# Two-scale attention with a top-1 expert layer: attention issued as a software pipeline over head pairs

## The chip, the cores and the metric

The kernel runs on one core of a Trainium2 chip. The metric is the device time of one execution in microseconds (us). The core has five engines with queues of their own: PE (matmuls; the loads of its stationary operand are listed as PEld), DVE and ACT (elementwise work, both reach PSUM), POOL (elementwise work on SBUF and indirect DMA) and SP (here only DMA issue). Each engine executes its own instructions in order and waits for others through semaphores.

## The reference

Inputs: q, k, v of shape 8 batches x 8 heads x 576 positions x 64, and the weights of 8 experts. Per head there are two attentions: one over sequences pooled by 4 (144 positions, full softmax), repeated by 4, and one local, in which a position sees the 7 positions around it. Their sum, as 4608 tokens of 512 channels, goes through a top-1 expert layer.

```python
q_d = q.reshape(B, H, Sd, 4, D).mean(axis=3)            # k_d, v_d likewise, Sd = 144
out_up = np.repeat(sm_attn(q_d, k_d, v_d), 4, axis=2)
mask = np.abs(pos[:, None] - pos[None, :]) < 4
scores = np.where(mask, scale * np.matmul(q, k.transpose(0, 1, 3, 2)), -1e9)
x = out_up + np.matmul(softmax(scores), v)              # then (B*S, H*D) = (4608, 512)
e_idx = np.argmax(x @ w_gate, axis=1)
h = np.maximum(x[mask] @ w1[e], 0.0); ye = h @ w2[e]
out[mask] = gate_w[mask, None] * sigmoid(x @ w_output_gate)[mask, e, None] * ye
```

## The kernel before

**Two stages.** The attention stage takes batches one after the other and, in a batch, 4 head pairs; after its last pair a batch is gated: its tokens are given an expert and a rank there and are scattered by indirect DMA to a buffer in HBM, `hx_xs`, with one region per expert. The expert stage then reads each region back (`xg`), transposes it, and runs two matmuls per expert. `hx_xs` is filled beforehand with zero rows from the tile `zt`, since the expert stage always reads 640 rows.

**A pair (attn_pair).** q and k of two heads are loaded (`f`), cast to fp16 on POOL (`s16`, line 177), and transposed on PE into PSUM (`tp`, L180); the same operand times a small pooling matrix `pb` gives the pooled q and k (`pool_ps`, L182). Copies bring both to SBUF (`sT` on DVE, L185; `qkd` on ACT, L188). Scores are computed transposed, keys on partitions. A matmul with the identity first writes the additive mask (`mk`) into PSUM (L195 with 456 columns in `pa`, L209 with 408 columns in `pbt`), then the q.k matmuls add to it (L199; L211, L213, L215). These have 64 contraction rows, since head 0 lies on partitions 0 to 63 and head 1 on 64 to 127. So a head has 864 score columns: 576 local and 2 x 144 pooled.

**Exp in two halves.** To keep near-fp32 precision with fp16 matmuls, exp is taken twice on ACT, once to fp32 (`E`, L217 and L219) and once to fp16 (`eh`, L218 and L220), and `el`, the difference of the two, is formed on POOL for head 0 (L222) and on DVE for head 1 (L224). v is split likewise into `vh` (POOL, L345) and `vl` (DVE, L346), for a whole batch ahead of its pairs. The pooled v (`pd`, L353) is the product of `pv` and these: 12 matmuls of 512 columns per batch.

**Values.** Per head, 27 matmuls of 64 or 65 columns accumulate into `po`: 5 local blocks (L231) times (eh.vh, eh.vl, el.vh), and two pooled blocks (L238), each over two key chunks, of 128 and of 16 contraction rows, times the same three products. The 65th column carries the row sum of the softmax; DVE takes its reciprocal (L243) and scales into `xo` (L244).

**Gate (once per batch).** Pooled rows are repeated by 6 DMAs from `xo` to `up` (L253, L256); DVE adds them (L258), ACT casts to `t_xh` (L259), POOL forms the low half `t_xl` (L260). PE transposes both for each of 5 token blocks (L265, L267), DVE copies (`xT`, L269), PE forms the logits `lg` (L271, L274); a chain of small operations on DVE and ACT gives positions (L278 to L328), and POOL issues 5 scatters (L330).

**What sets the order.** The program is written straight down, loop by loop; a list scheduler then orders the instructions of each engine from the program's order, its own estimates and the free buffers of the pools, and puts in the waits. [...]

## Time and profile before

| what | value |
|---|---|
| runs shown | 784.08, 785.86, 788.26 us; median 785.86 |
| the profiled execution's own time | 780.59 us |
| its span, first to last instruction | 778.8 us |
| busy: PE, DVE, ACT, POOL | 514.8, 289.9, 216.4, 334.8 us |
| mean granted clock of PE | 0.657 of full speed |
| first addition of `up` (L258) for batch 0, for batch 7 | 98.9 and 570.6 us |
| first transposes of the expert stage (L390) | 604.32 us |

The span is cut at the three last times: a beginning with the first batch, seven batches of equal build, the end of the last gate, and the expert stage. Engine times in the table are sums of instruction times; instructions of one engine can overlap on PE, where matmuls are pipelined, so there the distance from one start to the next is what counts. Where an engine is idle, the views say what it waited for.

### The profile page before, as it was taken

The page shows a single profiled execution, that of the slowest core. Times are in us where ns is not written, and L with a number is a line of the kernel's source. Part 1 is how long each engine was busy: PE and PEld are TensorE (multiplying, and loading weights), DVE is VectorE, ACT ScalarE, POOL GpSimd, SP SyncE. Part 2 cuts the span into 40 slices and gives each one's busy share as a digit, 9 for nine tenths or more (in the row PEclk, how much of TensorE's full clock was granted, in tenths as well). Part 3 has the DMA queues.
Part 4 walks back from the last instruction along what each step waited for, and adds up shares of the span by engine and source line. Part 5 has one row for each costly group of instructions (what it writes and reads, how often), then busy time and mean ns, then how long its engine had stood idle before and what let it go on. Part 6 is the DMA issues. An engine that isn't in the chain of part 4 may idle for free. (4 is left out here: it accounts for less than half of the span.)

```text
span 778.8 us, 12008 instructions
## 1 busy us (share of the span) xinstructions
PE 514.8 (66%) x4849; PEld 326.8 (42%) x4849; DVE 289.9 (37%) x577; ACT 216.4 (28%) x441; POOL 334.8 (43%) x269
## 2 busy tenths in 40 slices
PE   1339636946772793777379378547711999799994
PEld 1116324615542461453345156335411655455552
DVE  4015434444443544454354345242322222222220
ACT  0124114413321441332144133223310233233331
POOL 9235466714924662491476346026122133233222
PEclk9855555555565655555555555655555899899997
DMA  9999664471424235143332414201022289889411
GB/s 204 244 228 203 129 125 107 81 153 26 110 63 88 75 72 122 46 110 71 76 80 67 88 34 90 64 1 31 21 45 75 55 184 194 196 168 199 138 61 69
DMA packets 152562, 81.66 MB, mean 105 GB/s; under 512 B 121709, under 2 KB 140141, under 8 KB 152496
## 3 DMA queue, kind: packets, MB, share of 16 engines
q1 hardware_dynamic: 129584, 44.52, 27.5%
q0 software_dynamic: 17664, 30.98, 18.8%
q10 hardware_dynamic: 5248, 5.28, 2.3%
q8 instruction: 40, 0.66, 0.3%
q14 instruction: 26, 0.21, 0.1%
HBM read 68.23 MB, written 20.72 MB: 114 GB/s over the span
## 5 line engine op out<-in xcount | busy, mean ns | idle before, releaser
L345 POOL TENSOR_SCALAR t_vh<-vf 128x640 f16<-128x640 f32 x32 | 68.5, 2142 | 98.1 <-DMA f<-in_k_dram 64.3
L177 POOL CAST s<-f 96x768 f16<-96x768 f32 x64 | 66.1, 1045 | 98.7 <-PE pool_ps L182 59.2
L265 PE MATMUL tp<-id,t_xh 128*128 128x128 f16 x160 | 22.2, 303 | 100.1 <-ACT t_xh L259 100.1
L231 PE MATMUL po<-t_vh,el 128*128 128x65 f16 x320 | 57.5, 243 | 34.9 <-POOL el L222 34.2
L399 PE MATMUL pu<-xgT,w1sb 128*128 128x320 f16 x512 | 73.7, 306 | 1.8 <-DVE xgT L391 1.5
L260 POOL TENSOR_TENSOR t_xl<-xo,t_xh 120x2560 f16<-120x2560 f32 x8 | 40.2, 5028 | 71.4 <-ACT t_xh L259 60.1
L409 PE MATMUL py<-w2sb,hs 128*128 128x512 f16 x320 | 70.4, 379 | 0.0
L222 POOL TENSOR_TENSOR el<-E,eh 128x864 f16<-128x864 f32 x32 | 58.4, 1826 | 20.1 <-ACT eh L220 19.4
L412 POOL DMA_INDIRECT out_dram<-y,xg x40 | 39.2, 980 | 63.5 <-ACT y L411 61.7
L231 PE MATMUL po<-t_vh,eh 128*128 128x65 f16 x320 | 61.0, 244 | 7.6 <-ACT eh L218 6.7
L231 PEld LDWEIGHTS <-eh 128*128 128x128 f16 x640 | 54.6, 130 | 19.7 <-ACT eh L218 8.7
L238 PE MATMUL po<-vd1h,el 128*128 128x65 f16 (+1 forms) x256 | 62.0, 242 | 0.0
L238 PE MATMUL po<-vdl,eh 128*128 128x64 f16 (+1 forms) x256 | 61.5, 240 | 0.0
L180 PE MATMUL tp<-id,s 96*128 96x96 f16 x384 | 39.2, 255 | 33.6 <-POOL s L177 33.6
L399 PEld LDWEIGHTS <-w1sb 128*128 128x128 f16 x512 | 51.3, 100 | 23.4 <-issue 2.8
L231 PE MATMUL po<-vl,eh 128*128 128x64 f16 x320 | 60.7, 242 | 0.0
L238 PE MATMUL po<-vd1h,eh 128*128 128x65 f16 (+1 forms) x256 | 60.1, 235 | 0.0
L231 PEld LDWEIGHTS <-el 128*128 128x128 f16 x320 | 41.5, 130 | 40.9 <-POOL el L222 38.6
L217 ACT ACTIVATE E<-pa 128x456 f32<-128x456 f32 x64 | 35.8, 559 | 80.4 <-PE pa L199 50.1
L265 PEld LDWEIGHTS <-t_xh 128*128 128x128 f16 x160 | 14.3, 132 | 103.8 <-ACT t_xh L259 103.8
L185 DVE COPY sT<-tp 128x576 f16<-128x576 f16 x64 | 29.0, 454 | 64.4 <-PE tp L180 49.3
L330 POOL DMA_INDIRECT hx_xs<-t_xh,pos x40 | 43.2, 1080 | 20.5 <-issue 10.4
(117 smaller groups left out, 1035.1 us busy)
## 6 DMA issues: line engine op xcount, KB each, us to landing
vf<-in_v_dram SPq DMA_DIRECT2D x64, 160.0 KB, 3.4
f<-in_q_dram SPq DMA_DIRECT2D x64, 144.0 KB, 3.3
f<-in_k_dram SPq DMA_DIRECT2D x64, 144.0 KB, 3.4
w1sb<-in_moe_w_dram POOLq DMA_DIRECT2D x8, 1024.0 KB, 10.6
w2sb<-in_moe_w_dram POOLq DMA_DIRECT2D x8, 1024.0 KB, 11.0
up<-xo SPq DMA_DIRECT2D x32, 240.0 KB, 4.4
hx_xs<-zt ACTq DMA_DIRECT2D x8, 645.0 KB, 16.0
xg<-hx_xs SPq DMA_DIRECT2D x8, 645.0 KB, 4.9
```

Of the source, the lines that this page charges most:

```text
L177: nc.gpsimd.tensor_copy(s16, f.rearrange("p m h d -> p m (h d)"))
L180: nc.tensor.transpose(tp[:, 96 * m:96 * m + 96], s16[:, m, :], id16[0:96, 0:96])
L222: nc.gpsimd.tensor_tensor(el, E32, eh, op=ALU.subtract)
L231: mm = nc.tensor.matmul(po[:, t, 0:n], lhsT=a[:, c], rhs=bm[:, hh, t, 0:n], start=(a is eh and bm is vh), stop=(a is el), skip_group_check ...
L238: mm = nc.tensor.matmul(po[:, g, 0:n], lhsT=a[0:kn, c], rhs=bm[0:kn, kc, hh, 0:n], start=(kc == 0 and a is eh and bm is vdh), stop=(kc == ...
L260: nc.gpsimd.tensor_tensor(xl[0:BR], x, xh[0:BR, :, 0:Dm], op=ALU.subtract)
L265: nc.tensor.transpose(tp[:, c, :], xh[:, t, 128 * c:128 * c + 128], id16)
L330: ins = nc.gpsimd.indirect_dma_start(out=xs_dram.ap(), out_offset=bass.IndirectOffsetOnAxis(ap=pos[:, t:t + 1], axis=0), in_=xh[0:P, t, :] ...
L345: nc.gpsimd.tensor_scalar(vh[:, hs, :, 0:D], vf, scalar1=VS, scalar2=None, op0=ALU.mult)
L399: nc.tensor.matmul(pu[:, 0:c1 - c0], lhsT=w1sb[:, c, 128 * f:128 * f + 128], rhs=xgT[:, c, c0:c1], start=(c == 0), stop=(c == 3))
L409: nc.tensor.matmul(py, lhsT=hs[:, f, 128 * j:128 * j + 128], rhs=w2sb[:, f, :], start=(f == 0), stop=(f == NG - 1))
L412: ins = nc.gpsimd.indirect_dma_start(out=out_rows, out_offset=bass.IndirectOffsetOnAxis(ap=xgi[:, j, Dm // 2 + 1:Dm // 2 + 2], axis=0), in ...
```

## The change

The attention stage is rewritten over 32 units, a unit being a pair of heads. `load(u)` issues the loads and the casts, `prep(u)` splits v, transposes and pools q and k and pools v, `scores_a` and `scores_b` compute the 456 and the 408 score columns of both heads together, with the head in the inner loop, into a double bank each (tags SA and SB, one buffer), and `soft` follows them. The main loop issues, for unit u, the loads of u+3, the scores of u+1, the values of u and the preparation of u+2; the gate is cut into `gate1`, `gate2` and `gate3`, issued after the first, second and third unit of the next batch.

- In `soft`, exp to fp16 goes to `eh`, then exp to fp32 is written back in place into PSUM, and DVE subtracts `eh` from it. One instruction covers both heads (912 and 816 columns). The tile `E` and POOL's subtraction are gone.
- `vh` is formed on ACT. v is pooled per unit: 12 matmuls of 128 columns, and the second one's output has 128 rows in place of 16.
- In `values`, all products with `eh` come first, then those with `el`, so both key chunks of the pooled blocks are gone through twice per head.
- In the gate the addition of `up` goes from DVE to POOL, and two of five copies `xT` go to ACT. In the last batch it is done block by block.
- `tp`, `lg`, `rk`, the pooled v and both outputs of the transposes share the two banks of tag T.
- The fill of `hx_xs` goes from ACT's queue to SP's, behind the loads of the fourth unit. The weights of experts 0 to 2 are requested after units 10, 16 and 22, with a copy of one element that makes the request wait for that unit.

The expert stage is the same.

```diff
-    pv = cst.tile([128, NB, SD], F16)
+    pv = cst.tile([128, NB, 256], F16)
...
-    for r in range(E):
-        nc.scalar.dma_start(
...
+    def prefill():
+        for r in range(E):
+            nc.sync.dma_start(
+                xs_dram.ap()[r * REG:r * REG + 128 * CAPJ, :].rearrange("(j p) d -> p j d", p=128),
+                _ap(zt, [zt.ap[0], [0, CAPJ], [1, XW // 2]]))
...
+    def load_weights(e, after=None):
         w1sb = wpool.tile([128, 4, F], F16, tag="w1")
+        w2sb = wpool.tile([128, NG, Dm], F16, tag="w2")
+        if after is not None:
+            nc.gpsimd.tensor_copy(w1sb[0:1, 0, 0:1], after)
+            nc.gpsimd.tensor_copy(w2sb[0:1, 0, 0:1], after)
...
-    def attn_pair(b, hp, vh, vdh, vdl, xo, vl):
...
+    def load(u):
+        b, hp = u // NP, u % NP
+        s16 = []
         for i, src in enumerate((q, k)):
             f = sbA.tile([96, 6, 2, D], F32, tag=f"qk{i}", bufs=3)
             for h in range(2):
+                nc.sync.dma_start(f[:, :, h, :], src[b, 2 * hp + h].rearrange("(m p) d -> p m d", p=96))
+            t16 = sbA.tile([96, 6, 2 * D], F16, tag=f"qk16{i}")
+            nc.gpsimd.tensor_copy(t16, f.rearrange("p m h d -> p m (h d)"))
+            s16.append(t16)
+        vf = sbA.tile([128, 2, NB, D], F32, tag="vf", bufs=3)
+        for h in range(2):
+            s = v[b, 2 * hp + h]
+            nc.sync.dma_start(vf[:, h, :, :], _ap(s, [[D, 128], [W * D, NB], [1, D]]))
+        st[u] = {"s16": s16, "vf": vf}
+
+    def prep(u):
+        d = st[u]
+        s16, vf = d.pop("s16"), d.pop("vf")
+        vh = vh_s[u % 3]
+        vl = sbA.tile([128, 2, NB, D], F16, tag="vl", bufs=3)
+        nc.scalar.activation(vh[:, :, :, 0:D], vf, AF.Copy, scale=VS)
+        nc.vector.scalar_tensor_tensor(vl, in0=vf, scalar=VS, in1=vh[:, :, :, 0:D],
+                                       op0=ALU.mult, op1=ALU.subtract)
+        qkT = sbA.tile([128, 2 * S], F16, tag="qkT", bufs=3)
+        t1 = psA.tile([128, 1024], F16, tag="T", bufs=2)
+        t2f = psA.tile([128, 512], F32, tag="T", bufs=2)
+        t2 = t2f.bitcast(F16)
+        n1 = 960
+        for i in range(2):
             for m in range(6):
+                c = S * i + 96 * m
+                o = t1[:, c:c + 96] if c < n1 else t2[:, c - n1:c - n1 + 96]
+                nc.tensor.transpose(o, s16[i][:, m, :], id16[0:96, 0:96])
+        for i in range(2):
             for m in range(6):
+                c = 96 + SD * i + 24 * m
+                nc.tensor.matmul(t2f[:, c:c + 24], lhsT=s16[i][:, m, :], rhs=pb[0:96, 0:24],
+                                 start=True, stop=True)
+        nc.vector.tensor_copy(qkT[:, 0:n1], t1[:, 0:n1])
+        nc.vector.tensor_copy(qkT[:, n1:2 * S], t2[:, 0:2 * S - n1])
+        qkd = sbA.tile([128, 2 * SD], F16, tag="qkd", bufs=3)
+        nc.scalar.copy(qkd, t2f[:, 96:96 + 2 * SD])
+        vdh = vdh_s[u % 3]
+        vdl = sbA.tile([128, 2, 2, D], F16, tag="vdl", bufs=3)
+        pd = psA.tile([128, 2, 2, D], F32, tag="T", bufs=2)
+        mms = [(t, m) for t in range(NB) for m in (vh, vl)]
+        for i, (t, m) in enumerate(mms):
+            nc.tensor.matmul(pd[:, 0], lhsT=pv[:, t, 0:128], rhs=m[:, :, t, 0:D],
+                             start=(i == 0), stop=(i == len(mms) - 1), skip_group_check=True)
+        for i, m in enumerate((vh, vl)):
+            nc.tensor.matmul(pd[:, 1], lhsT=pv[:, NB - 1, 128:256], rhs=m[:, :, NB - 1, 0:D],
+                             start=(i == 0), stop=(i == 1), skip_group_check=True)
+        nc.scalar.copy(vdh[:, :, :, 0:D], pd)
+        nc.vector.tensor_tensor(vdl, pd, vdh[:, :, :, 0:D], op=ALU.subtract)
+        d.update(qT=qkT[:, 0:S], kT=qkT[:, S:2 * S], qd=qkd[:, 0:SD], kd=qkd[:, SD:2 * SD],
+                 vh=vh, vl=vl, vdh=vdh, vdl=vdl)
+        d["eh"] = sbA.tile([128, 2, ND], F16, tag="eh", name="eh", bufs=2)
+        d["el"] = sbA.tile([128, 2, ND], F16, tag="el", name="el", bufs=2)
+
+    def soft(d, ps, c0, c1):
+        n = c1 - c0
+        nc.scalar.activation(d["eh"][:, :, c0:c1], ps[:, :, 0:n], AF.Exp, scale=scale)
+        nc.scalar.activation(ps[:, :, 0:n], ps[:, :, 0:n], AF.Exp, scale=scale)
+        nc.vector.tensor_tensor(d["el"][:, :, c0:c1], ps[:, :, 0:n], d["eh"][:, :, c0:c1], op=ALU.subtract)
+    def scores_a(u):
+        d = st[u]
+        ps = psA.tile([128, 2, 512], F32, tag="SA")
         for h in range(2):
+            nc.tensor.matmul(ps[:, h, 0:NA], lhsT=id16, rhs=mk[:, 0:NA], start=True, stop=False,
                              skip_group_check=True)
+        for t in range(4):
+            for h in range(2):
+                r = slice(64 * h, 64 * h + 64)
+                nc.tensor.matmul(ps[:, h, Q0[t]:Q0[t] + QN[t]], lhsT=d["kT"][r, W * t:W * t + 128],
+                                 rhs=d["qT"][r, Q0[t]:Q0[t] + QN[t]], start=False, stop=True,
                                  skip_group_check=True)
+        soft(d, ps, 0, NA)
+    def scores_b(u):
+        d = st[u]
+        ps = psA.tile([128, 2, 512], F32, tag="SB")
         for h in range(2):
+            nc.tensor.matmul(ps[:, h, 0:NBt], lhsT=id16, rhs=mk[:, NA:ND], start=True, stop=False,
+                             skip_group_check=True)
+        for c0, c1, kk, k0, k1, qq in ((0, 120, "kT", W * 4, W * 4 + 128, d["qT"][:, NA:S]),
+                                       (120, 120 + SD, "kd", 0, 128, d["qd"]),
+                                       (120 + SD, NBt, "kd", 128, SD, d["qd"])):
+            for h in range(2):
+                r = slice(64 * h, 64 * h + 64)
+                nc.tensor.matmul(ps[0:k1 - k0, h, c0:c1], lhsT=d[kk][r, k0:k1], rhs=qq[r],
+                                 start=False, stop=True, skip_group_check=True)
+        soft(d, ps, NA, ND)
+
+    def values(u, h, xo):
+        d = st[u]
+        eh, el = d["eh"][:, h], d["el"][:, h]
+        hh = 2 * (u % NP) + h
+        po = psA.tile([128, NB + 2, 65], F32, tag="O", bufs=2)
+        mms = []
+        for e_, hi in ((eh, True), (el, False)):
             for t in range(NB):
                 c = slice(Q0[t], Q0[t] + 128)
+                mms.append((po[:, t, 0:65], e_[:, c], d["vh"][:, h, t, 0:65]))
+                if hi:
+                    mms.append((po[:, t, 0:D], e_[:, c], d["vl"][:, h, t, :]))
             for g, q0 in ((NB, 0), (NB + 1, 16)):
                 for kc, kn in ((0, 128), (1, 16)):
                     c = slice(S + SD * kc + q0, S + SD * kc + q0 + 128)
+                    mms.append((po[:, g, 0:65], e_[0:kn, c], d["vdh"][0:kn, kc, h, 0:65]))
+                    if hi:
+                        mms.append((po[:, g, 0:D], e_[0:kn, c], d["vdl"][0:kn, kc, h, :]))
+        for i, (o, a, m) in enumerate(mms):
+            nc.tensor.matmul(o, lhsT=a, rhs=m, start=(i == 0), stop=(i == len(mms) - 1),
+                             skip_group_check=True)
...
-    def gate(b, xo):
+    def gate1(b, parts):
...
-        nc.vector.tensor_tensor(x, x, up, op=ALU.add)
+        for t0, t1 in parts:
+            x = xo[0:BR, t0:t1, :]
+            nc.gpsimd.tensor_tensor(x, x, up[:, t0:t1], op=ALU.add)
+            nc.scalar.copy(xh[0:BR, t0:t1, 0:Dm], x)
+            nc.gpsimd.tensor_tensor(xl[0:BR, t0:t1], x, xh[0:BR, t0:t1, 0:Dm], op=ALU.subtract)
+    def gate2(b, ts):
+        xh, xl = xh_s[b % 2], t_xl
+        if ts[0] == 0:
+            lg_s[b] = psA.tile([128, NB, 4 * E], F32, tag="T", name="lg", bufs=2)
+        lg = lg_s[b]
+        for t in ts:
             tp = psA.tile([128, 8, 128], F16, tag="T", bufs=2)
             for c in range(4):
                 nc.tensor.transpose(tp[:, c, :], xh[:, t, 128 * c:128 * c + 128], id16)
             for c in range(4):
                 nc.tensor.transpose(tp[:, 4 + c, :], xl[:, t, 128 * c:128 * c + 128], id16)
             xT = sbA.tile([128, 8, 128], F16, tag="xT")
+            if t % 2:
+                nc.scalar.copy(xT, tp)
+            else:
+                nc.vector.tensor_copy(xT, tp)
...
+    def gate3(b):
...
-        rk = psA.tile([128, NB, E], F32, tag="M")
+        rk = psA.tile([128, NB, E], F32, tag="T", bufs=2)
...
+    xo_s, lg_s = {}, {}
+    NU = B * NP
+    late = {10: 0, 16: 1, 22: 2}
+    def late_weights(u):
+        if u in late:
+            load_weights(late[u], st[u]["vh"][0:1, 0, 0, 0:1])
+    for u in range(3):
+        load(u)
+    for u in range(2):
+        prep(u)
+    scores_a(0)
+    scores_b(0)
+    for u in range(NU + 5):
+        b, hp = u // NP, u % NP
+        if u == 1:
+            prefill()
+        if u + 3 < NU:
+            load(u + 3)
+        if u + 1 < NU:
+            scores_a(u + 1)
+        if u < NU:
+            if hp == 0:
+                xo_s[b] = sbA.tile([128, NB + 2, Dm], F32, tag="xo", name="xo")
+            values(u, 0, xo_s[b])
+        if u + 1 < NU:
+            scores_b(u + 1)
+        if u + 2 < NU:
+            prep(u + 2)
+        if u < NU:
+            values(u, 1, xo_s[b])
+            late_weights(u)
+        gb = b - 1
+        last = gb == B - 1
+        if gb >= 0:
+            if hp == 0:
+                gate1(gb, [(t, t + 1) for t in range(NB)] if last else [(0, NB)])
+            if (hp == 1 and not last) or (hp == 0 and last):
+                gate2(gb, [0, 1, 2, 3, 4])
+            if (hp == 2 and not last) or (hp == 0 and last):
+                gate3(gb)
+            if last:
+                break
```

The scheduler makes of this, at three places, the following. First PE, at the end of a batch. Before, behind the last values (`po`) come the pooled v of the next batch (`pd`) and then the gate's transposes (`tp`):

```order
L353 MATMUL pd_2545<-vl_2523,pv_102 128x512
L353 LDWEIGHTS pv_102
L353 MATMUL pd_2558<-t_vh_142,pv_102 16x512
L353 LDWEIGHTS pv_102
L353 MATMUL pd_2558<-vl_2523,pv_102 16x512
L265 LDWEIGHTS t_xh_135
L265 MATMUL tp_2364<-id16_61,t_xh_135 128x128
```

Now the first transposes of the gate of batch 3 stand between the values of units 18 and 19, four units after their batch, and values follow them at once:

```order
L298 MATMUL po_3846<-t_vd_135,el_3427 128x65
L331 LDWEIGHTS t_xh_152
L331 MATMUL tp_3629<-id16_61,t_xh_152 128x128
L331 LDWEIGHTS t_xh_152
L331 MATMUL tp_3629<-id16_61,t_xh_152 128x128
L331 LDWEIGHTS t_xh_152
L331 MATMUL tp_3629<-id16_61,t_xh_152 128x128
L331 LDWEIGHTS t_xh_152
L331 MATMUL tp_3629<-id16_61,t_xh_152 128x128
L298 LDWEIGHTS eh_3595
L298 MATMUL po_3964<-t_vh_137,eh_3595 128x65
```

So what PE waited for at a batch's end is asked for a batch later. Second, POOL around a gate. Before, the low half (L260), the scatters (L330) and the subtractions for exp (L222) stand between the casts:

```order
L222 TENSOR_TENSOR el_2267<-E32_2265,eh_2266 128x864
L345 TENSOR_SCALAR t_vh_133<-vf_3318 128x10x64
L260 TENSOR_TENSOR t_xl_151<-xo_1780,t_xh_135 120x2560
L177 CAST s16_2854<-f_2851 96x768
L330 DMA hx_xs<-t_xh_135,pos_2502 36864x258 x5
L222 TENSOR_TENSOR el_2621<-E32_2619,eh_2620 128x864
```

Now the subtractions are gone, the addition (L319) has come, and between the gate of one batch and the scatters of it lie five casts:

```order
L319 TENSOR_TENSOR xo_3332<-xo_3332,up_4244 120x2560
L187 CAST t16_4257<-f_4254 96x768
L321 TENSOR_TENSOR t_xl_159<-xo_3332,t_xh_145 120x2560
L187 CAST t16_4262<-f_4259 96x768
L187 CAST t16_4506<-f_4503 96x768
L187 CAST t16_4511<-f_4508 96x768
L187 CAST t16_4725<-f_4722 96x768
L187 CAST t16_4730<-f_4727 96x768
L402 DMA hx_xs<-t_xh_145,pos_4705 36864x258 x5
```

A cast that stands behind an addition or a scatter waits for it. Third, the beginning. Before, ACT's queue opens with the fill, ahead of everything that ACT computes:

```order
L145 DMA hx_xs<-zt 128x5x258 x8
L355 ACT_TABLE_LOAD
L355 CAST vd1h<-pd 128x8x64
L355 CAST vd1h<-pd 16x8x64
L188 CAST qkd<-pool_ps 128x288
L217 ACTIVATE E_270<-pa 128x456
```

Now it stands in SP's queue, behind the loads of the fourth unit and ahead of those of the fifth:

```order
L192 DMA vf<-in_v_dram 128x5x64 x2
L149 DMA hx_xs<-zt 128x5x258 x8
L185 DMA f<-in_q_dram 96x6x64 x2
L185 DMA f<-in_k_dram 96x6x64 x2
L192 DMA vf<-in_v_dram 128x5x64 x2
```

ACT's queue begins with its own work, and the loads from the fifth unit on are issued after the fill.

125 lines of the change are left out of this document (18 added, 107 removed).

## The prediction

> **What bounds the kernel now.** I first cut the span into stages. The columns are the stretch in us, its length, the busy time of PE, PEld, DVE, ACT and POOL (instructions in brackets), the granted clock of PE, the DMA share and GB/s.
>
> ```profile
> 98.90:570.60 471.70, 304.94 (x3359) 200.70 (x3359) 204.34 (x407) 138.35 (x292) 229.08 (x146) 0.56 0.35 75
> 570.60:604.30 33.70, 6.57 (x87) 5.68 (x88) 9.21 (x28) 3.06 (x4) 10.05 (x6) 0.50 0.18 52
> 604.30:778.80 174.50, 155.25 (x992) 93.83 (x992) 44.61 (x88) 55.49 (x104) 47.98 (x50) 0.94 0.63 140
> ```
>
> The cuts are the first and the last addition of the gate and the first transposes of the experts. Seven batches take 471.7 us, 67.4 each. In these PE is busy for 304.9 / 7 = 43.6, POOL 32.7, DVE 29.2, ACT 19.8. So no engine is full: PE idles 24 us per batch. The view of waits says for what:
>
> ```profile
> PE tp L265 <- ACT t_xh L259: 100.1, 8, 15.7
> ...
> PE tp L180 <- POOL s L177: 33.6, 6, 10.8
> ```
>
> These are 134 us, the beginning and the last batch included: the gate, 100.1 / 8 = 12.5 per batch, and the preparation behind it. PE stands at the gate's transposes, and nothing of the next batch is put ahead of them. The experts (174.5 us) are PE at nearly full clock and stay.
>
> **The clock decides what PE's work costs.** Inside a batch there are long stretches without idle time, and they run at half clock:
>
> ```profile
> 535.50:556.00 20.50, 20.43 (x232) 13.86 (x233) 8.46 (x17) 8.98 (x20) 8.59 (x7) 0.50 0.01 2
> ```
>
> It rises only where one dense piece fills some 3 us, such as the gate's transposes and logits, and goes again:
>
> ```profile
> 248.60:252.00 3.40, 3.04 (x48) 2.78 (x46) 2.01 (x4) 0.00 (x0) 0.00 (x0) 0.50 0.00 0
> 252.00:255.40 3.40, 2.79 (x63) 2.23 (x59) 3.05 (x9) 0.47 (x2) 0.00 (x0) 1.00 0.00 0
> ```
>
> [...] After the change the two dense pieces get thinner: the pooled v shrinks from 12 matmuls of 512 columns to 12 of 128, and the gate's blocks get waits between them (below). I take 0.50 for all of the attention stage.
>
> **The change, part by part: a unit on PE.** Prices at half clock, from the chain of waits (start, us):
>
> ```profile
> 541.94 0.77 PE pa L195 x2
> 542.71 0.34 PE pbt L209
> 543.05 0.82 PE po L231 x15
> 543.87 0.99 PE po L238 x12
> 544.86 0.50 PE pa L199 x8
> ...
> 545.78 0.59 PE tp L180 x6
> 546.38 0.15 PE pool_ps L182 x6
> ```
>
> Masks: 0.77 + 2 x 0.34 = 1.45. Scores: the eight of both heads take 0.50, and I give the six of the second bank, which now also come in turns of head 0 and head 1, 6/8 of that, 0.38. Transposes and pooling: 2 x 0.74 = 1.48. Values: 15 local matmuls take 0.82, or 0.055 each; the 12 pooled ones 0.99 because of steps between 128 and 16 contraction rows:
>
> ```profile
> 536.37 0.25 PE L238 MATMUL po<-vd1h,el 128*128 128x65 f16 x1
> 536.55 0.23 PE L238 MATMUL po<-vd1h,eh 16*128 16x65 f16 x1
> 536.60 0.24 PE L238 MATMUL po<-vdl,eh 16*128 16x64 f16 x1
> ```
>
> From 536.37 to 536.55 it is 0.18, to the next 0.05: a step costs 0.12 more. Before, a head has 4 such steps; with all eh products ahead of all el products it has 8. So a unit's values are 54 x 0.055 + 16 x 0.12 = 4.9, where they were 3.9: **this edit loses 1 us per unit, 31 in all.** [...] Pooled v, by a quarter of the 512 columns:
>
> ```profile
> 361.96 0.63 PE L353 MATMUL pd<-vl,pv 128*128 128x512 f16 x1
> 362.39 0.63 PE L353 MATMUL pd<-t_vh,pv 128*128 128x512 f16 x1
> ```
>
> 12 x 0.43 / 4 = 1.28. Together 1.45 + 0.50 + 0.38 + 1.48 + 4.9 + 1.28 = 10.0 us of PE per unit.
>
> **What lies beside it.** From the groups by form of POOL, DVE and ACT (busy time of all, mean ns of one):
>
> ```profile
> L177 POOL CAST s<-f 96x768 f16<-96x768 f32 x64 | 66.1, 1045 | 98.7 <-PE pool_ps L182 59.2 <-DMA f<-in_k_dram 18.2 <-issue 10.1
> L222 POOL TENSOR_TENSOR el<-E,eh 128x864 f16<-128x864 f32 x32 | 58.4, 1826 | 20.1 <-ACT eh L220 19.4 <-DMA f<-in_k_dram 0.2
> L330 POOL DMA_INDIRECT hx_xs<-t_xh,pos x40 | 43.2, 1080 | 20.5 <-issue 10.4 <-DVE more L373 9.5 <-ACT eh L220 0.6
> L260 POOL TENSOR_TENSOR t_xl<-xo,t_xh 120x2560 f16<-120x2560 f32 x8 | 40.2, 5028 | 71.4 <-ACT t_xh L259 60.1 <-DMA vf<-in_v_dram 11.3
> ...
> L244 DVE TENSOR_TENSOR xo<-po,rs 128x448 f32<-128x448 f32 x64 | 39.8, 622 | 1.6
> ...
> L217 ACT ACTIVATE E<-pa 128x456 f32<-128x456 f32 x64 | 35.8, 559 | 80.4 <-PE pa L199 50.1 <-POOL el L222 29.5
> L220 ACT ACTIVATE eh<-pbt 128x408 f16<-128x408 f32 x64 | 33.4, 522 | 0.0
> L219 ACT ACTIVATE E<-pbt 128x408 f32<-128x408 f32 x64 | 33.2, 519 | 36.6 <-PE pbt L215 36.5
> ```
>
> ACT: 456 and 408 columns take 559 and 519 ns, so a column makes 0.83 ns and the rest is 0.18; 912 cost 0.94 and 816 0.86; bounds are 0.56 (width free) and 1.12 (two old ones). Writing to PSUM shows nowhere; I take the same. Four exps are 3.6; with vh (640 columns, 0.7), two copies (0.8) and a quarter of the gate's 5, ACT has 6.3 us per unit. DVE: subtraction out of PSUM is priced by L244 (622 ns for 448), 1.1 + 1.0, bounds 1.0 and 2.5; with vl, copies, reciprocals and scaling about 6, and 1.8 for the gate. POOL: two casts (2.1) and a quarter of two gate passes of 5.03 (the addition priced as the subtraction of L260) and of five scatters (1.08 each and 0.3 between, 7): 6.4. L222 (1.83) falls away. All stay below 10.0, so PE covers them; were PE at full clock, DVE's 7.8 would be the bound.
>
> **Waits that are new.** SA and SB have one buffer, so the masks of the next unit wait for the subtraction of this one: two exps, subtraction and hand-overs of 0.2, 3.6 us. Between them PE has pooled v, values and transposes of 4 us: covered. The values' second part waits for exp of SB, which on ACT stands behind exp of SA twice and the copy of pooled v: I find 0.6 us uncovered (bounds 0 and 2). So 10.6 per unit, 42.4 for four.
>
> **The gate.** Its transposes, DMAs and POOL's passes now have four units to arrive, so the 100 and the 33 us of waits go. What is late next is its own copy: `lg` holds one of the two T banks until all five blocks are through, so `tp` has one bank, where blocks before followed each other every 1.06 us:
>
> ```profile
> 249.85 0.59 PE L265 MATMUL tp<-id,t_xh 128*128 128x128 f16 x4
> ...
> 250.90 0.69 DVE L269 COPY xT<-tp 128x1024 f16<-128x1024 f16 x1 [0.74 <-PE tp L267]
> 250.91 0.59 PE L265 MATMUL tp<-id,t_xh 128*128 128x128 f16 x4
> ```
>
> Three of five blocks now wait for their copy (0.69 on DVE, 0.18 + 1024 x 0.83 ns = 1.03 on ACT, 0.4 for hand-overs) with little between, 3 us (bounds 0 and 7). With 5 x 1.06 and 0.6 for the ranks a gate is 9. A batch is 42.4 + 9 = **52 us in place of 67.4**.
>
> **The two ends.** Before, ACT computes nothing until the fill is issued:
>
> ```profile
> 9.80 25.63 ACTq L145 DMA_DIRECT2D hx_xs<-zt  x8
> ```
>
> and the weights share the first 60 us of DMA. Now the first unit has the DMAs for itself: about 10 us to its first scores. The fill delays the loads of the fifth unit to about 45 us, where PE asks for them at about 50: covered; if not, up to 15 us. So the first batch's values are done at 10 + 4 x 10.6 + 3 for filling = 56, where they were at 98.9 - 9.5 = 89. At the other end:
>
> ```profile
> 570.55 2.83 DVE L258 TENSOR_TENSOR xo<-xo,up 120x2560 f32<-120x2560 f32 x1 [9.53 <-DMA up<-xo]
> ...
> 586.88 0.30 ACT lg L278
> ```
>
> From the last scaling to the addition it is 9.5, with the DMAs of `up` between. Then POOL does ten passes of 1.0, with the scatters of batch 6 (7 us) ahead of the last: 17; transposes and logits 2; from there to the experts as before, 604.3 - 586.9 = 17.4. That is 46, where it was 604.3 - 570.6 + 9.5 = 43.
>
> **Sum.** 56 + 7 x 52 + 46 + 174.5 = 640.5 of span, against 778.8. The profiled execution took 780.59, 1.8 more than its span, and the median of the runs is 0.7% above it: 642 and **647 us**.
>
> **The rivals.** (1) **The clock rises.** For it: the stretch from 252.00 kept 1.00 with only 2.79 us busy. Against: the 20 us at 0.50, and thinner dense pieces. PE's 10 us then halve, DVE's 7.8 bound a unit; a batch is 4 x 7.8 + 5 = 36: 44 + 7 x 36 + 46 + 174.5 = 516, or 522; with the clock up half the time 585. (2) **POOL is late.** Casts stand behind additions, low halves and scatters, 17 us per batch; for it, POOL already kept PE waiting 33.6 us at L180. Against: casts are asked for a unit and a half ahead, some 10 us of cover. Price 7 to 8 us per batch: 705. (3) **Slower: the score chain is not covered.** With one buffer for SA and SB each, if values never fall between exp and subtraction, PE waits out the chain: 0.94 + 0.94 + 0.4 + 0.86 + 0.86 + 1.0 and hand-overs of 0.8, 5.8 us per unit. A batch is 4 x 15.8 + 9 = 72, the sum 76 + 7 x 72 + 46 + 174.5 = 800, or 808. It decides from 14.8 us per unit on. Against: in the new order values stand between the score pieces.
>
> **How the numbers follow.** Forecast (PE at half clock bounds): 0.70, its own range 605 to 695 from the bounds of the waits (0 to 2 us per unit, 0 to 7 per gate), the steps and the fill, which will not all fall on one side. Rival 1: 0.14. Rival 2: 0.11. Rival 3: 0.05. The range of 8 in 10 runs from 578, half of rival 1, to 712, behind rival 2. What this kernel's measurement can tell from no change is about 0.5%; only rival 3 lies near or beyond it: faster 0.95, same 0.01, slower 0.04.
>
> **What would show it.** Right: mean clock near 0.50 between first batch and last, PE busy 90% there, batches 50 to 55 us apart, the steps' 0.18 twice as often, waits at `xT` between gate blocks, ACT computing before 12 us. Wrong: a clock above 0.65 there; idle PE in front of `T` transposes with POOL as releaser (2), or in front of the masks with DVE as releaser (3).

## The result and the profile after

The changed kernel takes 594.09 us (median of 4 runs, 591.17 to 601.84), the kernel before 785.8 us (4 runs). The ratio is 0.7546, with a 95% interval of 0.7508 to 0.7585: 24.5% less, about 192 us. The forecast was 647 us with a range from 578 to 712, so the time lies inside the range, 53 us below the forecast and outside its own narrower range of 605 to 695. Executions more than 1.5% above the fastest of their kernel are left out of a ratio that has an interval; three runs below keep too few without them, and have the ratio of all medians and no interval.

The stages of the changed kernel by the view of windows (columns as before: stretch, length, busy time of PE, PEld, DVE, ACT and POOL, granted clock, DMA share, GB/s). The first row holds six batches from one addition of the gate to the next:

```profile
67.92:344.06 276.14, 233.29 (x3025) 170.65 (x3022) 163.38 (x362) 137.21 (x202) 142.96 (x103) 0.69 0.72 143
344.06:367.97 23.91, 20.94 (x289) 15.39 (x288) 14.91 (x30) 12.41 (x17) 10.65 (x3) 0.81 0.01 2
367.97:410.60 42.63, 10.01 (x134) 7.72 (x135) 14.15 (x45) 7.29 (x14) 21.85 (x20) 0.50 0.33 85
410.60:591.50 180.90, 156.60 (x992) 94.64 (x992) 44.72 (x88) 55.49 (x104) 48.29 (x50) 0.92 0.60 134
```

A batch takes 276.14 / 6 = 46.0 us where it took 67.4. PE is busy for 38.9 of them and idle for 7, where it was idle for 24. POOL, DVE and ACT have 24, 27 and 23 us, so PE is the fullest engine, as foreseen. Its granted clock is 0.69 in this row, where it was 0.56, and not 0.50; above 0.65 was the prediction's own sign that its likeliest case is wrong.

The view of waits shows what became of the two large ones, 100.1 us for the high half and 33.6 us for the casts:

```profile
PE tp L480 <- DMA xg<-hx_xs: 25.4, 3, 14.8
...
PE lg L340 <- DVE xT L338: 14.6, 17, 3.4
PE tp L333 <- POOL t_xl L321: 13.0, 6, 3.2
...
PE lg L340 <- ACT xT L336: 11.4, 10, 1.2
```

Neither is in the list any more. What is late next is what the prediction named: the copies `xT` between the gate's blocks, 14.6 + 11.4 us, and beside them POOL's low half, 13.0.

The last scaling of the first batch is the eighth of line 302 (timeline of DVE, the first and the eighth):

```profile
23.25 0.62 DVE L302 TENSOR_TENSOR xo<-po,rs 128x448 f32<-128x448 f32 x1
...
49.58 0.62 DVE L302 TENSOR_TENSOR xo<-po,rs 128x448 f32<-128x448 f32 x1
```

The last one of all and the first transposes of the experts stand in the chain of waits:

```profile
366.94 1.03 DVE xo L302 x2
...
410.60 1.88 PE tp L480 x16
```

So the four terms of the sum came out like this (us):

| term | before | predicted | measured | from |
|---|---|---|---|---|
| first batch's values end | 89 | 56 | 50.2 | 49.58 + 0.62 |
| seven batches | 472 | 364 (52 each) | 317.8 (45.4 each) | 367.97 - 50.2 |
| last value to experts | 43 | 46 | 42.6 | 410.60 - 367.97 |
| experts | 174.5 | 174.5 | 180.9 | 591.5 - 410.6 |
| span | 778.8 | 640.5 | 591.5 | |

46 of the 49 us by which the sum was too long are in the seven batches.

### The profile page after: what moved, and what is told of

Read it like the earlier page. It is cut to its first block, busy times and chain, and to the rows that moved or that the text cites. A ratio compares the mean times of both kernels' runs of the same rounds, so it can differ in the third digit from the quotient of the medians.

```text
span 591.5 us, 12472 instructions
## 1 busy us (share of the span) xinstructions
PE 477.0 (81%) x5137; PEld 327.9 (55%) x5137; DVE 278.6 (47%) x604; ACT 244.3 (41%) x381; POOL 245.4 (41%) x227
## 4 chain that ended last, share of the span: by engine, by line
PE 32%; issue 27%; POOL 18%; DMA 8%; DVE 6%; ACT 3%; SPq 3%; POOLq 1%; ACTq 0%
PE po L298 10%; POOL t_xl L321 5%; POOL out_dram L502 5%; POOL xo L319 3%; PE pd L229 3%; DMA xg<-hx_xs 3%; PE t L214 3%; PE tp L333 2%; POOL hx_xs L402 2%; PE ps L252 2%; POOL t L187 2%; PE pu L489 2%; DMA out_dram<-y,xg 2%; PE tp L331 2%; DVE xT L338 2%
## 5 line engine op out<-in xcount | busy, mean ns | idle before, releaser
L187 POOL CAST t<-f 96x768 f16<-96x768 f32 x64 | 56.8, 908 | 99.8 <-issue 55.3
L298 PEld LDWEIGHTS <-eh 128*128 128x128 f16 (+1 forms) x1152 | 61.2, 107 | 28.2 <-issue 5.8
L244 ACT ACTIVATE eh<-ps 128x912 f16<-128x912 f32 x64 | 57.1, 892 | 33.1 <-PE t L214 10.4
L246 DVE TENSOR_TENSOR el<-ps,eh 128x912 f16<-128x912 f32 x64 | 66.8, 1047 | 7.6 <-ACT ps L245 7.2
L321 POOL TENSOR_TENSOR t_xl<-xo,t_xh 120x2560 f16<-120x2560 f32 (+1 forms) x12 | 41.0, 3422 | 44.3 <-ACT t_xh L320 31.7
L245 ACT ACTIVATE ps<-ps 128x912 f32<-128x912 f32 x64 | 57.1, 892 | 0.0
L298 PEld LDWEIGHTS <-el 128*128 128x128 f16 (+1 forms) x576 | 41.9, 106 | 23.5 <-issue 7.2
L319 POOL TENSOR_TENSOR xo<-xo,up 120x2560 f32<-120x2560 f32 (+1 forms) x12 | 45.6, 3798 | 16.5 <-DMA up<-xo 10.1
L494 DVE TENSOR_SCALAR hs<-pu 128x320 f16<-128x320 f32 x64 | 31.5, 492 | 44.4 <-PE pu L489 36.7
L298 PE MATMUL po<-t_vd,eh 128*128 128x65 f16 (+1 forms) x256 | 49.6, 213 | 0.4 <-issue 0.4
```

The costliest lines, as they stand in the source:

```text
L187: nc.gpsimd.tensor_copy(t16, f.rearrange("p m h d -> p m (h d)"))
L244: nc.scalar.activation(d["eh"][:, :, c0:c1], ps[:, :, 0:n], AF.Exp, scale=scale)
L245: nc.scalar.activation(ps[:, :, 0:n], ps[:, :, 0:n], AF.Exp, scale=scale)
L246: nc.vector.tensor_tensor(d["el"][:, :, c0:c1], ps[:, :, 0:n], d["eh"][:, :, c0:c1], op=ALU.subtract)
L298: nc.tensor.matmul(o, lhsT=a, rhs=m, start=(i == 0), stop=(i == len(mms) - 1), skip_group_check=True)
L319: nc.gpsimd.tensor_tensor(x, x, up[:, t0:t1], op=ALU.add)
```

## The experiments

Each run is compared by its ratio to the kernel before, which ran on the same chip beside it; the changed kernel stands at 0.7546. A difference of 0.01 in this ratio is 7.9 us.

### Which parts of the pipeline bring the gain

**The gate's parts at once.** All three parts of a gate follow the batch's last unit:

```diff
-            if (hp == 1 and not last) or (hp == 0 and last):
-                gate2(gb, [0, 1, 2, 3, 4])
-            if (hp == 2 and not last) or (hp == 0 and last):
-                gate3(gb)
+                gate2(gb, [0, 1, 2, 3, 4])
+                gate3(gb)
```

> The three parts of a batch's gate are issued together, right after the batch's last unit, in place of one part after each of the next three units; units stay two and one ahead. Theory D (the delay is what hides the gate's transfers and passes, 12.5 us per batch before): PE waits at the gate's transposes again, for the additions and the low half (5.6 + 2.3 + 5.0 us) less the work that the units ahead still give, 4 to 10 us per batch, 620 to 665 us. Rival E (the units ahead alone cover it, since the scheduler moves the gate's matmuls behind other work by itself): within 1% of 594.

Measured: 658.65 us, ratio 0.8432 (0.8354 to 0.8510), 70 us more than the changed kernel. Theory D holds. Units two and one ahead don't cover the gate by themselves: PE stands at its transposes, ranks and copies again, in the view of waits up to 430 us:

```profile
PE tp L333 <- POOL t_xl L321: 25.5, 7, 4.5
PE pd L229 <- DVE qkT L220: 18.3, 13, 2.7
PE lg L340 <- DVE xT L338: 16.5, 21, 0.8
PE lg L340 <- ACT xT L336: 15.9, 14, 1.2
PE rk L365 <- DVE oh L363: 12.8, 7, 1.8
PE tp L331 <- ACT t_xh L320: 12.2, 3, 7.4
```

**Scores at their own unit.** In the main loop `scores_a(u)` and `scores_b(u)` are issued right ahead of `values(u, 0)`:

```diff
-        if u + 1 < NU:
-            scores_a(u + 1)
         if u < NU:
+            scores_a(u)
+            scores_b(u)
```

> The changed kernel (16 steps), but a unit's scores are issued right ahead of its own values, not one unit ahead; preparation stays two units ahead and the gate late. Theory O (scores one unit ahead are what covers the chain of two exps and a subtraction, my prediction's third rival): PE waits 2 to 5 us per unit, 64 to 160 us more, 660 to 750. Rival P (preparation ahead and the late gate do most, since the scheduler puts pooled v and transposes of the next units into the gap): below 640.

Measured: 633.57 us beside 786.79 us for the kernel before, a ratio of 0.805; 40 us more than the changed kernel (33 by its two shortest executions), or 1.2 us per unit. That is below the band of theory O and inside that of rival P. Not all of it is the chain of exps: in the six batches from 64.48 to 376.06 us PE waits 12.5 us for the low half of v (line 202, up to 8.3 us for one operation in place of 0.8) and 9.9 for DVE's scaling, where the changed kernel has 2.0 for both. These long operations of DVE end with POOL's addition; rows of such a pair stand below, with the low half in SBUF. So the slow rival of the prediction (5.8 us per unit) was overpriced even for a kernel without this part.

**The start as before.** The fill on ACT's queue and the weights of experts 0 to 2 are issued ahead of everything:

```diff
-            nc.sync.dma_start(
+            nc.scalar.dma_start(
                 xs_dram.ap()[r * REG:r * REG + 128 * CAPJ, :].rearrange("(j p) d -> p j d", p=128),
...
+    prefill()
     for u in range(3):
         load(u)
+    for e in range(3):
+        load_weights(e)
...
-    late = {10: 0, 16: 1, 22: 2}
+    late = {}
```

> The changed kernel (16 steps), but the fill of the buffer is issued at the start on ACT's queue and the weights of experts 0 to 2 are requested at the start, as in the kernel before. Theory Q (my prediction's start term: ACT computes nothing until the fill is issued, at 35 us in the trace of before, and the first units' loads share the transfers with 5 MB of fill and 6 MB of weights): the first batch's last value ends at 75 to 90 us in place of 58, 610 to 625 us. Rival R (what is transferred first is paid later anyway, since the transfers are full until 100 us either way): within 1.5% of 594.

Measured: 617.0 us, ratio 0.7832 (0.7757 to 0.7906), 22 us more, inside the band of theory Q. The profile shows its mechanism, ACT's next copy behind the issue of the fill (timeline of ACT):

```profile
10.15 32.21 ACTq L149 DMA_DIRECT2D hx_xs<-zt  x6
42.40 0.40 ACT L223 CAST qkd<-t2f 128x288 f16<-128x288 f32 x1 [31.92 <-DMA hx_xs<-zt]
```

The table's first term fell by 39 us (89 to 50). In this profile, of the longest of the five executions (631.44 us), it is back at 96.7 us, later than theory Q's 75 to 90. So the start alone accounts for the whole of that term, and yet the kernel loses 22 us and not 46: part of what the start gains is paid later anyway, which is what rival R held. How large that part is, one profile of a long execution does not tell.

**The low half in SBUF.** exp to fp32 goes to a tile in SBUF, as before the change, and DVE subtracts there:

```diff
-        nc.scalar.activation(ps[:, :, 0:n], ps[:, :, 0:n], AF.Exp, scale=scale)
-        nc.vector.tensor_tensor(d["el"][:, :, c0:c1], ps[:, :, 0:n], d["eh"][:, :, c0:c1], op=ALU.subtract)
+        E32 = sbA.tile([128, 2, 512], F32, tag="E32", name="E32", bufs=2)
+        nc.scalar.activation(E32[:, :, 0:n], ps[:, :, 0:n], AF.Exp, scale=scale)
+        nc.vector.tensor_tensor(d["el"][:, :, c0:c1], E32[:, :, 0:n], d["eh"][:, :, c0:c1], op=ALU.subtract)
```

> The fp32 exp goes to a tile in SBUF, as in the kernel before, and the subtraction on DVE reads it there; it is no longer written back into PSUM. Theory F (where exp is written does not matter to ACT, and DVE is not what PE waits for): ACT's 0.89 us stays, the subtraction goes from 1.05 towards 1.4 by the 1398 ns for 864 columns of before, the score banks come free one subtraction earlier, and the time is within 1.5% of 594. Rival G (taking the low half in PSUM is a gain of its own, since DVE's reads of SBUF stand against POOL's): the subtraction takes 1.5 us or more and the time rises by 10 us or more.

Measured: 621.93 us, ratio 0.7977 (0.7907 to 0.8047), 34 us more. Theory F falls, rival G holds. The groups by form show that ACT's 0.93 us stayed, and that the mean of the 816-column subtraction nearly doubled. Changed kernel, then this run:

```profile
L246 DVE TENSOR_TENSOR el<-ps,eh 128x912 f16<-128x912 f32 x32 | 34.9, 1092 | 2.8 <-ACT ps L245 2.8
L246 DVE TENSOR_TENSOR el<-ps,eh 128x816 f16<-128x816 f32 x32 | 32.1, 1002 | 4.8 <-ACT ps L245 4.4
```

```profile
L247 DVE TENSOR_TENSOR el<-E,eh 128x816 f16<-128x816 f32 x32 | 62.9, 1964 | 5.5 <-ACT E L246 5.2
L247 DVE TENSOR_TENSOR el<-E,eh 128x912 f16<-128x912 f32 x32 | 39.9, 1247 | 3.3 <-ACT E L246 3.0
```

The mean hides two kinds. Most of the subtractions take 1 us (median 1.07); a few last to the end of POOL's pass beside them. In this run's timelines of DVE and of POOL:

```profile
210.48 8.72 DVE L247 TENSOR_TENSOR el<-E,eh 128x816 f16<-128x816 f32 x1
219.13 1.44 DVE L202 SCALAR_TENSOR_TENSOR vl<-vf,t_vh 128x640 f16<-128x640 f32 x1
```

```profile
211.15 1.59 POOL L187 CAST t<-f 96x768 f16<-96x768 f32 x2
212.71 5.56 POOL L320 TENSOR_TENSOR xo<-xo,up 120x2560 f32<-120x2560 f32 x1
```

DVE's subtraction from SBUF ends at 219.2, which is 0.93 us, about its usual length, behind the end of POOL's addition at 218.27. PE waits for it, in this run's view of waits:

```profile
PE po L299 <- DVE el L247: 26.5, 6, 6.4
```

In the changed kernel this wait is 0.2 us. With the operand in PSUM the longest of 64 took 1.1 us, though 16 of them stand beside a pass of POOL of 5.0 to 5.6 us (L319, L321):

```profile
L246 DVE TENSOR_TENSOR el<-ps,eh x64: 992/1032/1108, 16.8 to 362.5; 128x912 f16<-128x912 f32 x32, 128x816 f16<-128x816 f32 x32
```

So taking the low half in PSUM is worth 34 us here, and not for the 1.0 us that it takes by itself, but for the up to 8.72 us that it takes from SBUF beside POOL's passes. What holds the two together is not shown: their ends stand a usual length apart, and their starts do not tell which held up the other, since the subtraction is recorded from 210.48, ahead of POOL's casts at 211.15. The prediction gave this part no price of its own.

### What the clock follows

**More dense work.** Three useless matmuls of 512 columns ahead of each unit's pooled v, into the bank that it then overwrites:

```diff
+        for _ in range(3):
+            nc.tensor.matmul(pdf, lhsT=id16, rhs=mk[:, 0:512], start=True, stop=True,
+                             skip_group_check=True)
```

> Three useless matmuls of 512 columns and 128 rows are put ahead of each unit's pooled v, into the bank that the pooled v then overwrites: 1536 columns per unit more, 1.28 us at half clock, 0.64 at full. Nothing else is changed. Theory A: nearly every window now passes the mark, the clock between 44 and 368 us goes to 0.9 or above, and the time stays at 575 to 600 us in spite of the added work. Rival B (the clock follows PE's busy share, or something outside the kernel): clock unchanged at 0.71 and 32 x 0.9 = 29 us more, about 620.

Measured: 627.5 us, ratio 0.8008 (0.7932 to 0.8083), 36 us more; the clock between the first and the seventh addition (65 to 379 us) is 0.73. The time is near what rival B expected, but the run doesn't decide between the two. The added work moved the other engines' orders as well, and in this stretch PE now waits 39.8 us for DVE's scaling, which was 2.0 in the six batches of the changed kernel:

```profile
PE po L302 <- DVE xo L306: 39.8, 6, 9.2
```

41 of the 83 windows whose clock can be told run at full clock, where theory A wanted nearly all. But the wait alone is as large as the loss, and while PE waits, no columns go through. Five of the six are 6.7 to 9.2 us long, and each follows a small operation of the gate on DVE (L396) that lasts until POOL's addition ends. The first of them, in the timelines of DVE and POOL:

```profile
118.12 6.67 DVE L396 TENSOR_SCALAR t_xh<-tok_i 120x5 int32<-120x5 int32 x1 [4.64 <-DMA hx_xs<-t_xh,pos]
124.71 0.61 DVE L306 TENSOR_TENSOR xo<-po,rs 128x448 f32<-128x448 f32 x1
```

```profile
119.17 5.58 POOL L323 TENSOR_TENSOR xo<-xo,up 120x2560 f32<-120x2560 f32 x1
```

**Eight steps in place of 16.** Per head all products with 128 rows stand together, then those with 16:

```diff
-            for g, q0 in ((NB, 0), (NB + 1, 16)):
-                for kc, kn in ((0, 128), (1, 16)):
+            for kc, kn in ((0, 128), (1, 16)):
+                for g, q0 in ((NB, 0), (NB + 1, 16)):
```

> Only the order of the value matmuls changes: per head all products with 128 contraction rows stand together and all with 16 rows together, so a unit has 8 steps between 128 and 16 rows in place of 16. Theory A (the granted clock of a 3.41 us window follows how many full-height columns PE streamed in the window before; about 3,100 are needed): the 1 us that the steps leave PE without columns is what keeps many windows below the mark. Without it the clock between 44 and 368 us rises from 0.71 to above 0.80, and the time falls to 555 to 570 us. Rival B (the steps cost their plain 0.12 us at half clock and 0.09 at full, the clock does not care): 32 x 8 x 0.10 = 26 us less, 565 to 572, clock in that stretch within 0.03 of 0.71. Rival C (PE does not bound the units, the gate and the transfers do): within 1% of 594.

Measured: 573.06 us, ratio 0.7349 (0.7279 to 0.7418): 15 us less than the changed kernel by the ratios, with their intervals 7 to 24. A batch falls from 46.0 to 261.54 / 6 = 43.6:

```profile
65.56:327.10 261.54, 200.87 (x2995) 153.99 (x2993) 188.82 (x362) 136.18 (x200) 144.11 (x102) 0.73 0.74 151
```

PE has 5.4 us less to do per batch, but its idle time went up by 3, to 10 us per batch. Theory A asked for a clock above 0.80 and rival B for 26 us: neither came out in full. What was taken off PE is partly lost to a wait for DVE: in the six batches PE waits 21.8 us for the scaling, which was 2.0, behind a low half of v (line 202) that lasts up to 7.33 us in place of 0.83 beside POOL's addition.

**The same instructions, fewer rows.** To take the order out of the question, a last run keeps every instruction in its place on all engines and changes the contraction rows alone:

```diff
-            nc.tensor.matmul(pd[:, 0], lhsT=pv[:, t, 0:128], rhs=m[:, :, t, 0:D],
+            nc.tensor.matmul(pd[:, 0], lhsT=pv[0:96, t, 0:128], rhs=m[0:96, :, t, 0:D],
...
-            nc.tensor.matmul(ps[:, h, 0:NA], lhsT=id16, rhs=mk[:, 0:NA], start=True, stop=False,
+            nc.tensor.matmul(ps[:, h, 0:NA], lhsT=id16[0:96], rhs=mk[0:96, 0:NA], start=True, stop=False,
```

and likewise for the second half of the mask, the products with `vl`, and the local ones of `el`.

> The changed kernel with every instruction in the same place on every engine and of the same number of columns; only some matmuls have 96 contraction rows in place of 128: the mask's, the pooled v's, those of vl and the local ones of el. The attention's values are changed by it (keys on rows 96 to 127 lose their mask and part of their products). Columns weighted by rows fall from about 8,000 to 6,900 per unit; PE's busy time and its columns stay. Theory A (a window is granted the full clock when about 3,100 columns weighted by rows went through PE in the 3.41 us before): almost no window rises any more, the clock between 44 and 368 us falls from 0.71 to 0.50 to 0.58, a batch goes from 46 to 49 to 51 us, the time to 615 to 635 us. Rival B (the clock goes by busy time or by columns whatever their rows, or from outside): clock within 0.04 of 0.71, time within 1.5% of 594.

Measured: 748.97 us as a whole, which can't be read: the changed values send other numbers of tokens to the experts, and passes are added behind the eighth expert. The attention stage can. Its first and seventh addition:

```profile
66.94 5.59 POOL L319 TENSOR_TENSOR xo<-xo,up 120x2560 f32<-120x2560 f32 x1 [2.52 <-DMA up<-xo]
...
363.58 5.60 POOL L319 TENSOR_TENSOR xo<-xo,up 120x2560 f32<-120x2560 f32 x1
```

A batch takes 296.64 / 6 = 49.4 us in place of 46.0, inside the band of theory A, and the first transposes of the experts begin at 434.06 in place of 410.60, 23 us later. The granted clock of the view of windows doesn't show it, though: it has 0.72 for the same stretch, since it reads 1.00 for everything ahead of the first recorded change, at 168.00 us. The matmuls themselves tell otherwise. In a window that it calls 1.00, products of 64 and 65 columns stand 0.05 us apart, and in the changed kernel, where its records have 1.00 from 304.08 on, 0.03:

```profile
88.03 0.24 PE L298 MATMUL po<-t_vh,eh 128*128 128x65 f16 x1
88.08 0.25 PE L298 MATMUL po<-vl,eh 96*128 96x64 f16 x1
88.14 0.24 PE L298 MATMUL po<-t_vh,eh 128*128 128x65 f16 x1
```

```profile
308.24 0.20 PE L298 MATMUL po<-vl,eh 128*128 128x64 f16 x1
308.27 0.19 PE L298 MATMUL po<-t_vh,eh 128*128 128x65 f16 x1
308.30 0.19 PE L298 MATMUL po<-vl,eh 128*128 128x64 f16 x1
```

By these distances between equal matmuls, taken per window of 3.41 us, 32 of 82 windows in the six batches of the changed kernel run at full clock, as its records have it too, and 9 of 88 with fewer rows. The order and the columns did not change, and PE's busy share rose from 84 to 91%; so between these two runs the clock followed neither busy time nor columns as such, and rival B falls. Columns weighted by rows fit, by the count below. (The edit changes the values in the products as well; that it is the rows and not the values was not tested apart, but the same count fits the runs with unchanged values alike.)

Where the two sides part can be read from the traces. The clock of the changed kernel changes only at points of a grid of 3.41 us (54.91, 109.52, 153.89, 177.78, 211.92, 300.67, 304.08 and 317.73 us among them). The trace holds every matmul of the program, so the columns of each window can be counted, a matmul of 64 rows as half and so on. The count rests on an assumption that no record shows by itself, that a matmul streams 0.06 us behind its recorded start; without it, two of the 81 windows of the changed kernel fall on the wrong side, by up to 3%. For the batches between the first and the last full addition, and every window whose next one has a clock that the distances show:

```
run                windows   highest count,     lowest count,
                             next window half   next window full
kernel before      108       3,078              3,142
changed kernel      81       3,065              3,097
more dense work     82       3,033              3,109
8 steps             73       3,057              3,156
fewer rows          87       3,029              3,071
```

In none of the five runs do the two sides overlap; across the runs they do by 7, with 3,078 before a half window and 3,071 before a full one. So in these runs the mark lies at about 3,070 weighted columns, whether the counted window itself is at half clock or at full: in the changed kernel the highest count before a half window is 3,065 and 2,954, the lowest before a full one 3,128 and 3,097. At half clock a window has room for some 4,100 columns, an estimate from matmuls of 512 columns in the kernel before, which start at 88.88, 89.31, 89.73 and 90.16 us, 0.427 apart; the mark is three quarters of that. Columns without the weight do not fit: 7 of the 81 windows are then on the wrong side of the best mark. Nor does busy time: 16 windows of the changed kernel are busy throughout and stay at half. Counted like this, the long stretch before the change (535.5 to 556.0) had 2,260 to 2,910 per window, in spite of PE being busy for 20.43 of its 20.50 us.

### What is left

**The addition back on DVE**, with 8 steps:

```diff
-            nc.gpsimd.tensor_tensor(x, x, up[:, t0:t1], op=ALU.add)
+            nc.vector.tensor_tensor(x, x, up[:, t0:t1], op=ALU.add)
```

> As the run with 8 steps (573 us), and the gate's addition goes back from POOL to DVE. Theory H (POOL's long passes over SBUF hold up DVE's operations that read SBUF: the low half of v took 7.33 us once in place of 0.83 while the addition of 5.6 us ran, and PE then waits for xo, 21.8 us in six batches): the addition takes 2.8 us on DVE, the long times of line 202 remain only under the low half's 5.0 us, the waits for xo shrink below 10 us, and the time falls by 8 to 20 us to 553 to 565. Rival J (DVE is the busier engine, 72% in those batches, and 2.8 us more per batch delay its copies): 570 to 585.

Measured: 568.97 us beside 786.79, a ratio of 0.723, against 0.735 with 8 steps alone; the spread of the four runs (561.89 to 573.54) is as wide as the difference, so a gain is likely and not shown. The longest operation of line 202 (the low half of v) went from 7.3 to 5.1 us, and that of 5.1 is beside POOL's low half; the waits for `xo` are gone from the list, while 12.1 us for `el` are new.

**Copies cut in two**, with 8 steps:

```diff
-            if t % 2:
-                nc.scalar.copy(xT, tp)
-            else:
-                nc.vector.tensor_copy(xT, tp)
+            nc.vector.tensor_copy(xT[:, 0:5], tp[:, 0:5])
+            nc.scalar.copy(xT[:, 5:8], tp[:, 5:8])
```

> As the run with 8 steps (573 us), and each of the gate's copies xT is cut in two, 640 columns on DVE and 384 on ACT at the same time, in place of whole ones on the two engines in turn. The gate's transposes and copies share one bank, so a block takes transposes + copy + logits; the copy goes from 0.69 or 1.02 to about 0.5. Theory K (this chain stands on PE's path, 20 us of waits in six batches): 5 x 0.35 = 1.8 us per gate and as much at the end, 8 x 1.8 = 14 us, 557 to 565. Rival L (between the blocks other matmuls stand anyway): within 0.7% of 573.

Measured: 574.33 us, ratio 0.7314 (0.7230 to 0.7397), no difference to 0.7349. Rival L: the waits at `lg` are as long as they were (19.6 + 7.7 us), now for the later of two halves.

**The fill spread over eight units**, with 8 steps:

```diff
-        if u == 1:
-            prefill()
+        if 1 <= u <= 8:
+            prefill((u - 1,))
```

> As the run with 8 steps (573 us), and the eight DMAs that fill the buffer are spread, one after the loads of each unit from the fourth on, in place of all behind the loads of the fourth. Theory M (the fill stands ahead of the next units' loads on SP and PE has nothing between about 80 and 95 us; the transfers as such would be in time): the pause shrinks by 5 to 12 us, 560 to 568. Rival N (the 16 DMA engines are full until 100 us in any order, share above 1.0): within 0.7% of 573, the pause only moves; the scatters of the first batch then wait longer.

Measured: 601.77 us, ratio 0.7669 (0.7595 to 0.7743), 25 us slower than with 8 steps alone. Neither theory foresaw that. The last two regions are filled only behind the scatters of the first batch (whose rows there are lost), and on SP's queue the loads of v stand behind them. In this run's timeline of SP:

```profile
84.18 0.86 SPq L185 DMA_DIRECT2D f<-in_k_dram  x2
110.71 0.95 SPq L149 DMA_DIRECT2D hx_xs<-zt  x2
111.75 5.89 SPq L192 DMA_DIRECT2D vf<-in_v_dram  x2
```

SP issues nothing from 85 to 110 us, until POOL's scatters of 102.0 to 108.4 are through; its own view of waits has 25.1 us for them in one wait. Whether a spread that ends ahead of the first scatter gains anything wasn't tried.

**The gate one unit later**, with 8 steps and the addition on DVE: its second part after the third unit, its third after the fourth.

```diff
-            if (hp == 1 and not last) or (hp == 0 and last):
+            if (hp == 2 and not last) or (hp == 0 and last):
                 gate2(gb, [0, 1, 2, 3, 4])
-            if (hp == 2 and not last) or (hp == 0 and last):
+            if (hp == 3 and not last) or (hp == 0 and last):
                 gate3(gb)
```

> The run with 8 steps and the addition on DVE (569 us), and the gate's transposes are issued one unit later (after the third unit of the next batch) and its ranks and scatters after the fourth. Theory S (PE still stands at the gate because POOL's low half comes too late, waits of 10.6 us at the transposes of the low half and 9.0 at the ranks): these waits go and the time falls by 8 to 20 us, 549 to 561. Rival T (what stops PE there is the chain of five blocks through one bank, wherever it stands): within 1% of 569.

Measured: 573.19 us, ratio 0.7309 (0.7246 to 0.7371). No gain, rival T in time; the wait for the low half even rose, from 10.6 to 16.1 us in the views of waits. POOL's pass moved with the rest, so that it is late again in the new place: in the third to the seventh batch it starts 3.6 to 6.5 us later behind its batch's last scaling than in the run with the gate one unit earlier.

**Four steps per unit**, with the addition on DVE: the products with 16 rows of `eh` and `el` stand next to each other.

```diff
+        loc(eh, True)
+        pool(eh, True, 0, 128)
+        pool(eh, True, 1, 16)
+        pool(el, False, 1, 16)
+        loc(el, False)
+        pool(el, False, 0, 128)
```

(`loc` gives a head's local products, `pool` those of one key chunk.)

> The run with 8 steps and the addition on DVE (569 us), with 4 steps per unit between 128 and 16 rows: the products of 16 rows with eh and with el stand next to each other. Theory A (below the mark of about 3,100 columns the clock halves, each step removed moves windows over it): 32 x 4 x 0.1 = 13 us and some clock, 548 to 558. Rival U (PE idles a fifth of a batch by now, so its own work is no longer what counts; the products of 16 rows with el also wait for the second subtraction): within 1% of 569, or slower.

Measured: 565.29 us (552.22 to 568.96) beside 786.1, a ratio of 0.719. Against 0.723 with 8 steps that is within the spread: rival U. It has the lowest median of the study, 28 us below the changed one by the ratios; by the steps of the study, only the first of its edits (16 to 8 steps, 15 us) is shown to be a gain.

## Why the prediction was right or wrong

**Direction, bound and order of size: right.** PE was to bound the new stage, and does, with 85% busy. The gate's waits of 100 and 33 us went, and the gate issued at once brings 70 us back. The late terms were named correctly: copies between the gate's blocks. The tail (46 against 42.6) was near. The start (56 against 50.2) had the right cause, ACT's queue behind the fill. That the time lies in the wide range is not owed to the mechanism of the forecast: the lower end, 578, was taken from half of rival 1.

**The step that failed: "I take 0.50 for all of the attention stage."** Of the excess of 49 us 46 lie in the batches. With fewer rows, where 79 of 88 windows stay at half clock and the order of PE's work is the same, a batch takes 49.4 us; the prediction had 52 for half clock. So of the 6 us between 52 and the measured 46.0 the clock makes at least 3.4, and up to 2.6 are prices that were too high. Of these 0.6 are a slip in the sum: 42.4 + 9 is 51.4 and was taken as 52, which makes 4 us over seven batches. Rival 1 gave 585 for a clock that is up half the time; 32 of 82 windows and 594 us came close to it. The likeliest case should have lain between the forecast and that.

**Why the step failed.** It read the clock from busy time: 20.43 us busy at 0.50 seemed to show that no filling of PE helps. Busy time counts a matmul with 16 rows like one with 128 (0.23 and 0.25 us at 543.97 and 543.79 in the kernel before), and it counts the 0.12 us of a step between them. By weighted columns that stretch was below the mark, by 5 to 26%. A unit of the changed kernel has some 8,000 weighted columns and a gate 5 x (1,024 + 192), so a batch has 38,000; over 46.0 us, or 13.5 windows, that is a mean of 2,830, close under 3,070, so that each window with a little more goes over. The 16 windows of the changed kernel that were busy throughout and stayed at half clock show the same: what went with the clock in these runs was rows times columns, not busy time.

**The two dense pieces.** "After the change the two dense pieces get thinner" was true of the instructions and led the wrong way: spread among the units, the same columns can, by these counts, bring many windows over the mark. This is argued from the counts above; no run tests it by itself.

**The steps: right in sign, too large in effect.** The distance of 0.18 us (119.06 to 119.24 in the changed kernel, where two of equal rows stand 0.05 apart) is there 16 times per unit, but the edit was to cost 31 us, and undoing it gives 15 (7 to 24). With 8 steps PE has 5.4 us less to do per batch, but idles 10 us in place of 7, since DVE's scaling is late behind POOL's addition; so part of what is taken off PE only becomes waiting.

**The exps: right for ACT.** 0.94 and 0.86 us were forecast, 0.93 and 0.85 measured (here the in-place ones):

```profile
L245 ACT ACTIVATE ps<-ps 128x912 f32<-128x912 f32 x32 | 29.7, 929 | 0.0
L245 ACT ACTIVATE ps<-ps 128x816 f32<-128x816 f32 x32 | 27.3, 854 | 0.0
```

The subtraction was forecast at 1.1 and 1.0 and took 1.09 and 1.00. What the prediction missed is that the same subtraction from SBUF costs 34 us more in all, and that DVE's other operations on SBUF last longer beside POOL's addition, which the change brought (the low half of v 7.33 us in place of 0.83 with 8 steps): it priced POOL and DVE each by itself.

**Rivals 2 and 3: rightly small.** No wait of PE for a cast is in the changed kernel's list, where rival 2 had 7 to 8 us per batch; the nearest, in front of the pooling matmuls (line 218), is 6.6 us in the whole stage and has no releaser in the profile. Without scores ahead a unit is 1.2 us longer, not 5.2, and part of that is POOL's addition.

**The experts: not seen.** 180.9 in place of 174.5 us, with PE waiting for `xg` three times (25.4 us) where it was two (20.0). The third wait is 5.5 us in front of the sixth expert, with the DMA engines busy for 0.95 of the time from 500 to 531 us; why it falls there now was not tested.
